# A fused attention, gated and slot-expert kernel: another load plan, other hand-over steps in the last pass, another order of the tail

## The chip, the cores and the metric

The kernel runs on one core of a Trainium2 chip as one launch. The metric is device time in microseconds (us) of an execution. Engines are named as in the profile: PE (matmul; PEld is its weight load), DVE (vector), ACT (scalar), POOL (GpSimd) and SP, which here only issues DMAs.

## What is computed

Three layers in a chain, all in fp32, cut from the reference (4 sequences of 448 rows, 12 heads of 64, so 1792 tokens of width 768):

```python
# 1 talking-heads attention: heads are mixed before and after the softmax
scores = scale * q @ k.T                       # (4, 12, 448, 448)
scores = einsum('bhij,hg->bgij', scores, w_pre)
attn = softmax(scores)                         # max subtracted, EPS in the sum
attn = einsum('bhij,hg->bgij', attn, w_post)
x = (attn @ v)                                 # -> (1792, 768)
# 2 gated layer; its weights come as 64-bit floats
h = x @ w_in                                   # (1792, 2048)
x = (h - tanh(h)) @ w_out
# 3 soft mixture: 8 experts of 4 slots each
logits = x @ phi                               # (1792, 32)
slot_in = softmax(logits, axis=0).T @ x        # (32, 768)
for e in range(8):
    h = relu(slot_in[e] @ w1[e])               # w1[e]: 768 x 1024
    slot_out[e] = h @ w2[e]                    # w2[e]: 1024 x 768
out = softmax(logits, axis=1) @ slot_out       # (1792, 768)
```

## The kernel before, in words

**Attention (talking_heads, to about 450 us).** The rows of scores are cut into 16 chunks (120, 120, 120 and 88 rows a sequence) and those into 184 steps of up to ten rows. Scores of a chunk go to a tile S; SP then fetches the rows of one step over all heads into a tile D (L312, 210 KB), four steps ahead of its use, into six buffers. Every second step PE mixes two D by w_pre (pm, L321), ACT makes the exponentials, and PE mixes and transposes them back (tm, L364). SP's other DMAs are written into a plan, at steps of their own: loads of k, q and v (load_k, load_q, load_v) and the conversion of w_in and w_out from 64-bit floats to fp32 in 56 pieces (load of 384 KB, arithmetic on ACT, DVE and POOL, store of 192 KB). The plan keeps a tally of work per step: `fetch` gives a load a span of steps and a cost, and the load goes to the step with the least tally of "dma" around it; `due` spreads the conversion pieces. SP issues in the order of the steps, all on one queue.

**Gated layer (moe_and_slots, to about 790 us).** Four passes over the tokens (512, 512, 512 and 256), each with 16 steps (NF), one per 128 columns of h. A step is 18 matmuls hp (L831) in six groups (c = 0 to 5); other work hangs on these groups as hooks, `on(c, ...)`, where KD = 6 means behind the last. A step's h goes through ACT and DVE (gate_act, gate_first, gate_last; result g), and turn_g transposes the g of two steps before (PE gt, ACT copy) into a quad buffer; the quads of a pass are summed over the tokens by the slot weights es (slot_sum, PE sp) in the pass that follows. logits, mix_t, slot_exp and slot_turn make es. LAST is the first step of the last pass.

**Buffers for expert weights.** Each of 32 loads of 1536 KB needs a home; `give` adds one to the list and `load_expert` fills it, in the order of `queue`. In the last pass homes come free as tiles of the gated layer are done with: two at its start, three at step 5 (two ring buffers of the weights and three quads, released together), one at step 14; loads there are cut into pieces (load_piece), one or two a step. After the pass every home comes from a load that PE has used up.

**Tail.** Behind the last pass stand the last gates, slot sum, the slot inputs (si), their transposes (sip, from every sixth column) and the experts: hidden(e) makes h, finish(e) copies h (ACT), transposes it (tz, from every eighth column) and takes the maximum with 0; slot_out(e, part) adds to so in two banks, one per half of the output columns. Five experts load w2 in two parts by rows, three (by_column) by halves of the columns, these last of all. slot_mix makes S4 of a half, output(hf) multiplies 14 tiles of 128 tokens and stores them in groups of four, four, four and two (768, 768, 768 and 384 KB).

## Time and profile before

| | us |
|---|---|
| median of three runs | 896.32 (896.07 to 898.48) |
| profiled execution, its own time | 903.9 |
| span of the profiled execution, first to last instruction | 902.1 |
| PE busy in the span | 828.4 |
| DVE, ACT, POOL busy | 554.9, 572.7, 249.0 |

The profile is one execution with the hardware profiler on, so its time is compared with its own parts, and the runs' median with other runs. A wait is the idle time of an engine just before an instruction, put down to what ended it. The clock is the share of full speed that TensorE was granted, the DMA share the mean busy share of 16 DMA engines.

### The profile page before, as it was taken

The numbers are of one execution on the slowest core, as the hardware profiler recorded it, in microseconds if no ns is written. First come the engines' busy times: TensorE is split into PE (matmuls) and PEld (weight loads), VectorE is DVE, ScalarE is ACT, GpSimd is POOL, SyncE is SP. The second block draws the span as 40 slices with busy tenths as digits, with TensorE's granted clock in tenths as the row PEclk, the third lists the DMA queues.
The fourth block names the chain that finished last, engine by engine and source line by source line (L and its number), as shares of the span: only waits on it lengthen the run. The fifth ranks groups of instructions, "written<-read, shape, count | busy, mean of one in ns | idle before, by whom it ended". The sixth has DMA issues, their size and how long they took to land.

```text
span 902.1 us, 28586 instructions
## 1 busy us (share of the span) xinstructions
PE 828.4 (92%) x11760; PEld 586.2 (65%) x11760; DVE 554.9 (62%) x1177; ACT 572.7 (63%) x1347; POOL 249.0 (28%) x430
## 2 busy tenths in 40 slices
PE   8878988989988898989999999999999999999995
PEld 6556665656655666766776767767776777964543
DVE  4456766658667576858467886566766776820104
ACT  4757877768877688878666775546664666820013
POOL 6244334424433344434303453000000003700000
PEclk9979999989999999999999999999999999997997
DMA  6889888886898877875669976588755456999997
GB/s 137 225 210 234 229 214 222 224 222 205 217 213 226 225 215 205 246 211 180 203 217 362 379 270 211 199 312 325 300 210 175 161 183 225 319 382 419 416 371 255
DMA packets 145590, 224.53 MB, mean 249 GB/s; under 512 B 60916, under 2 KB 126516, under 8 KB 142132
## 3 DMA queue, kind: packets, MB, share of 16 engines
q1 hardware_dynamic: 142112, 209.83, 74.6%
q10 hardware_dynamic: 3348, 12.87, 3.7%
q8 instruction: 93, 1.52, 0.7%
q14 instruction: 37, 0.30, 0.1%
HBM read 147.96 MB, written 36.18 MB: 204 GB/s over the span
## 4 chain that ended last, share of the span: by engine, by line
PE 61%; DMA 13%; ACT 10%; DVE 8%; issue 6%; SPq 1%; POOL 1%; ACTq 0%; POOLq 0%; DVEq 0%
PE hp L831 21%; DMA D<-S 9%; PE pm L321 6%; PE tm L364 5%; PE sc L287 5%; PE vx L403 4%; ACT e L333 4%; PE h L1320 3%; DVE mx L325 3%; PE gt L902 2%; PE so L1361 2%; PE tz L1340 2%; PE lgp L986 2%; ACT S L295 2%; PE sp L1068 1%
## 5 line engine op out<-in xcount | busy, mean ns | idle before, releaser
L333 ACT ACTIVATE e<-pm,mx 128x448 f32<-128x448 f32 x184 | 115.2, 631 | 89.1 <-DVE mx L325 85.7
L325 DVE TENSOR_REDUCE mx<-pm 128x1 f32<-128x448 f32 x184 | 106.1, 618 | 83.1 <-PE pm L321 83.0
L831 PE MATMUL hp<-xa,rg 128*128 128x512 f32 x576 | 153.0, 405 | 0.6 <-ACT xa L814 0.4
L364 PEld LDWEIGHTS tm<-wk,e 64*56 64x56 f32 x5888 | 111.8, 132 | 59.4 <-issue 37.0
L321 PE MATMUL pm<-D,wpre 64*64 64x448 f32 (+2 forms) x736 | 117.0, 573 | 20.6 <-DMA D<-S 18.1
L364 PE MATMUL tm<-wk,e 64*56 64x60 f32 x5888 | 121.1, 220 | 12.9 <-issue 11.1
L831 PEld LDWEIGHTS hp<-xa,rg 128*128 128x128 f32 x576 | 102.3, 188 | 29.9 <-issue 10.5
L295 ACT ACTIVATE S<-sc 120x448 f32<-120x448 f32 (+1 forms) x186 | 91.4, 551 | 14.2 <-DMA D<-S 5.3
L287 PE MATMUL sc<-khi,qT 64*120 64x448 f32 (+1 forms) x384 | 84.1, 399 | 8.8 <-DVE xs L413 5.5
L339 POOL TENSOR_SCALAR rv<-ss 128x2 f32<-128x2 f32 x92 | 24.5, 266 | 238.1 <-ACT e L333 207.9
L350 POOL TENSOR_SCALAR wk<-wpost,rv 128x60 f32<-128x60 f32 x184 | 85.3, 494 | 16.2 <-DVE rv L343 14.8
L403 PE MATMUL vx<-aT,vn 128*64 128x120 f32 (+1 forms) x1536 | 86.1, 265 | 1.9 <-issue 1.4
L788 POOL TENSOR_TENSOR rg<-rg 128x384 fp32r<-128x384 f32 x24 | 24.0, 1013 | 209.4 <-DVE rg L785 200.4
L403 PEld LDWEIGHTS vx<-aT,vn 128*64 128x64 f32 x1536 | 75.6, 139 | 8.8 <-issue 4.0
L378 ACT ACTIVATE aT<-tm 128x480 f32<-128x480 f32 x144 | 75.9, 592 | 2.2 <-PE tm L364 2.2
L851 ACT ACTIVATE sq<-hp 128x512 f32<-128x512 f32 (+1 forms) x62 | 32.8, 529 | 68.8 <-PE hp L831 68.7
L862 DVE SCALAR_TENSOR_TENSOR qd<-qd,sq 128x512 f32<-128x512 f32 (+1 forms) x61 | 37.6, 616 | 61.7 <-ACT mk L858 53.8
L831 PE MATMUL hp<-xb,rg 128*128 128x512 f32 x288 | 74.8, 405 | 0.0
L321 PEld LDWEIGHTS pm<-D,wpre 64*64 64x64 f32 (+2 forms) x736 | 25.8, 133 | 59.7 <-DMA D<-S 23.2
L287 PEld LDWEIGHTS sc<-khi,qT 64*120 64x120 f32 (+1 forms) x384 | 46.6, 177 | 25.5 <-PE tm L364 8.0
L831 PEld LDWEIGHTS hp<-xb,rg 128*128 128x128 f32 x288 | 52.0, 188 | 16.6 <-issue 6.3
L71 POOL TENSOR_TENSOR fa<-fa,f 128x384 f32<-128x384 f32 x56 | 57.4, 1025 | 7.2 <-DVE rv L343 3.4
(198 smaller groups left out, 1403.6 us busy)
## 6 DMA issues: line engine op xcount, KB each, us to landing
ex<-in_moe_w_dram SPq DMA_DIRECT2D x24, 1536.0 KB
D<-S SPq DMA_DIRECT2D x144, 210.0 KB
rg<-wis SPq DMA_DIRECT2D x36, 768.0 KB
f<-in_moe_w_in_dram SPq DMA_DIRECT2D x32, 384.0 KB
wis<-rg ACTq DMA_DIRECT2D x16, 768.0 KB
f<-in_moe_w_out_dram SPq DMA_DIRECT2D x24, 384.0 KB
rg<-wi SPq DMA_DIRECT2D x19, 384.0 KB
wi<-fa SPq DMA_DIRECT2D x32, 192.0 KB
```

Of the source, the lines that this page charges most:

```text
L71: eng.tensor_tensor(out=out, in0=bits(a), in1=bits(p), op=ALU.add)
L287: nc.tensor.matmul(xs[e][0][:ni], lhsT=qT[n][s, l, p, :ni], rhs=kt[s], start=(i == 0), stop=(i == 2))
L295: nc.scalar.activation(out=dst, in_=xs[e][0][:ni], func=ACTF.Copy)
L321: nc.tensor.matmul(xs[x][64 * i:64 * i + 64], lhsT=wpre[k0:k1], rhs=d[i][k0:k1], start=True, stop=True)
L325: nc.vector.tensor_reduce(out=mx[:, x:x + 1], in_=xs[x], op=ALU.max, axis=AX.X, negate=True)
L333: nc.scalar.activation(out=es[x], in_=xs[x], func=ACTF.Exp, bias=mx[:, x:x + 1], accum_out=ss[:, x:x + 1])
L350: nc.gpsimd.tensor_scalar(out=wk, in0=wpost, scalar1=rv[:, x:x + 1], scalar2=None, op0=ALU.mult)
L364: nc.tensor.matmul(xs[i][64 * z:64 * z + JH, x, c], lhsT=es[x][h, j:j + JH], rhs=wks[x][h], start=True, stop=True)
L378: nc.scalar.activation(out=out[:, :, c0:c0 + m].rearrange("p a (x i) -> p a x i", x=2), in_=x, func=ACTF.Copy)
L403: nc.tensor.matmul(x[64 * e:64 * e + 64, i, :ni], lhsT=nat_v[b, h // NP][:, h % NP, c, :], rhs=a[:, c, h, :ni], start=(c == 0), stop=(c == ...
L831: nc.tensor.matmul(hp, lhsT=r32(w[:, m, hl, cs]), rhs=r32(x_of(b, c, l)), start=(c == 0 and i == 0), stop=(c == KD - 1 and i == 2))
L862: nc.vector.scalar_tensor_tensor(out=qd, in0=qd, scalar=TG_E, in1=sq, op0=ALU.add, op1=ALU.mult)
```

## The change

Four things. The plan of attention's loads is made anew: all fetches are placed first and with larger costs, and the conversion pieces get due steps from the rest. In the last pass the ring buffers (one tile now) come free at step 3 and the quads at step 4, with slot sums, logits and one turn_g moved among the hooks; six experts load w2 by rows and two by columns. The transposes tz and sip read contiguous columns, since ACT and DVE write their sources in the other order (w2's rows are counted to suit). And the tail's order is new: slot_mix and output are generators that are taken forward in parts.

The diff, cut to its core:

```diff
-                fetch(max(t - 30, 3), t - 6, 0.45, load_k, chunks[m + 1][0], p)
+                fetch(max(t - 30, 3), t - 6, 1.3, load_k, chunks[m + 1][0], p)
-            fetch(max(2, t0 - 12), t0 - 8 if t0 > 12 else max(2, t0 - 7), 0.7, load_q, m)
+            fetch(max(2, t0 - 12), t0 - 8 if t0 > 12 else max(2, t0 - 7), 2.0, load_q, m)
+    for b in range(NB):
+        s0 = start[b * NC // NB]
+        fetch(s0 - 12 if b else 4, s0 + 8 if b else 13, 2.7, load_v, b, 0)
+        fetch(s0 + (T_LAG + 10 if b else 8), s0 + 15, 2.7, load_v, b, 1)
...
     pieces = box["early"]
+    first, last = 2, NS - D_AHEAD - 17
+    taken = [sum(load["dma"][:s + 1]) for s in range(NS)]
+    rate = (taken[last] + 2.1 * len(pieces)) / (last - first)
+    dues = []
+    for i in range(len(pieces)):
+        s = next(s for s in range(first, NS) if s >= last or taken[s] + 2.1 * (i + 1) <= rate * (s - first + 1))
+        dues.append((s + first + i * (last - first) // len(pieces)) // 2 + 6)
...
-        due = 6 + i * (NS - D_AHEAD - 17) // len(pieces)
+        due = dues[i]
...
-    rgs = [xep.tile([128, RU], FP32, tag=f"rg{i}", name="rg") for i in range(2)]
+    rgs = rgp.tile([128, 2 * RU], FP32, tag="rgs", name="rg")
...
+    def by_column(e):
+        return e >= NE - 2
...
-    def by_column(e):
-        return e >= NE - 3
...
-                src = w2[e].rearrange("(p a) f -> p a f", p=128)
+                src = w2[e].rearrange("(h p a) f -> p h a f", h=2, p=128)
...
+        elif kind == "e" and part > 1 and by_column(e):
+            for h in range(2):
+                nc.sync.dma_start(out=dst[:, h * (n // 2):(h + 1) * (n // 2)], in_=src[:, h])
...
-        on(4 if t > LAST + 2 else 2, turn_g, u)
+        on(5 if t == LAST + 1 else 4 if t > LAST + 2 else 2, turn_g, u)
...
-            on(3, logits, b - 1, NQ - 1)
-            on(4, logits_out, b - 1)
+            on(3 if b < NPASS - 1 else 5, logits, b - 1, NQ - 1)
+            on(4 if b < NPASS - 1 else 5, logits_out, b - 1)
...
-        if b and f in (4, 5):
+        if b == NPASS - 1 and f in (3, 4):
+            on(KD, slot_sum, b - 1, 2 * f - 6, 2 * f - 4)
+        elif 0 < b < NPASS - 1 and f in (4, 5):
             on(3, slot_sum, b - 1, 2 * f - 8, 2 * f - 6)
...
-            if f == 5:
+            if f == 3:
+                give(rgp.tile([128, EXB], FP32, tag="rgs", name="ex"))
+            if f == 4:
                 firsts.close()
                 zp = whole.enter_context(tc.tile_pool(name="m_z", bufs=1, reuse_waits="tile"))
-                for i in range(3):
+                for i in range(2):
                     give(zp.tile([128, EXB], FP32, tag=f"z{i}", name="ex"))
...
-            load_piece(2 if f < 5 or f > NF - 3 else 1)
+            load_piece(2 if f < 4 or f > NF - 3 else 1)
...
-    nc.vector.tensor_copy(out=siS[:, :HALF], in_=si[0])
-    nc.scalar.activation(out=siS[:, HALF:], in_=si[1], func=ACTF.Copy)
+    siS = siS.rearrange("p (c m) -> p c m", c=KD)
+    nc.vector.tensor_copy(out=siS[:, :, :64], in_=si[0].rearrange("p (m c) -> p c m", c=KD))
+    nc.scalar.activation(out=siS[:, :, 64:], in_=si[1].rearrange("p (m c) -> p c m", c=KD), func=ACTF.Copy)
...
-        nc.tensor.matmul(sp[:, c, :], lhsT=siS[:, c::KD], rhs=seld, start=True, stop=True)
+        nc.tensor.matmul(sp[:, c, :], lhsT=siS[:, c], rhs=seld, start=True, stop=True)
...
-        nc.scalar.activation(out=hs, in_=hp, func=ACTF.Copy)
+        nc.scalar.activation(
+            out=hs.rearrange("p (a m) -> p a m", m=128), in_=hp.rearrange("p (m a) -> p a m", m=128), func=ACTF.Copy)
...
-        for fc in range(KF1):
-            for hf in range(2):
-                nc.tensor.matmul(
-                    tz[64 * hf:64 * hf + 64, fc, :], lhsT=hs[:, fc::KF1], rhs=sela[:, e, hf, :],
-                    start=True, stop=True)
+        for a in range(n):
+            nc.tensor.matmul(
+                tz[:, a].rearrange("p h s -> p (h s)"), lhsT=hs[:, a * 128:(a + 1) * 128],
+                rhs=sela[:, e].rearrange("p h s -> p (h s)"), start=True, stop=True)
...
-        nc.scalar.activation(out=s4[0:64], in_=x[0:64], func=ACTF.Copy)
+        nc.vector.tensor_copy(out=s4[0:64], in_=x[0:64])
...
-    slot_mix(0)
-    slot_out(NE - 3, 1)
-    output(0)
+    mix = slot_mix(0)
+    next(mix)
+    idle = p1.tile([128, 128], FP32, tag="h1", name="warm")
+    for _ in range(3):
+        nc.tensor.matmul(idle, lhsT=ident, rhs=ident, start=True, stop=True)
+    next(mix)
     slot_out(NE - 2, 1)
+    part = output(0, (OG, OG, OG, 2))
+    for _ in range(2 * OG):
+        next(part)
     slot_out(NE - 1, 1)
-    slot_mix(1)
-    output(1)
+    mix = slot_mix(1)
+    next(mix)
+    for _ in range(OG):
+        next(part)
+    next(mix)
+    for part in (part, output(1, (2, OG, OG, OG))):
+        for _ in part:
+            pass
```

**The order on SP, at the start of attention.** D<-S rows are the fetches for the steps, kn, qn and vn loads of k, q and v, and f loads of conversion pieces. Before:

```order
L312 DMA D<-S 120x1x448 x7
L94 DMA f_436<-in_moe_w_in_dram 128x3x256
L312 DMA D<-S 120x1x448
L88 DMA f_461<-in_moe_w_out_dram 128x768
L164 DMA kn<-in_k_dram 112x8x64
L312 DMA D<-S 120x1x448 x2
L94 DMA f_519<-in_moe_w_in_dram 128x3x256
L180 DMA qn<-in_q_dram 88x12x64
L312 DMA D<-S 120x1x448 x2
L174 DMA vn<-in_v_dram 56x6x256 x2
L312 DMA D<-S 120x1x448 x2
```

And of the change, for the same fetches:

```order
L312 DMA D<-S 120x1x448 x7
L180 DMA qn<-in_q_dram 88x12x64
L312 DMA D<-S 120x1x448 x2
L174 DMA vn<-in_v_dram 56x6x256 x2
L312 DMA D<-S 120x1x448 x2
L164 DMA kn<-in_k_dram 112x8x64
L312 DMA D<-S 120x1x448 x2
```

Ahead of the 13th fetch stood three conversion loads, one k, one q and a pair of v; of these the conversion loads now come later. Farther on, the pair of v that stood behind the 97th fetch stands behind the 87th.

**The order on PE, in the first steps of the last pass.** hp<-xc are its products, gt the transposes of turn_g, lgp the logits, lT mix_t. Before:

```order
L831 MATMUL hp<-xc,rg 128x256 x6
L902 MATMUL gt<-ident,g 128x128 x4
L831 MATMUL hp<-xc,rg 128x256 x18
L902 MATMUL gt<-ident,g 128x128 x4
L831 MATMUL hp<-xc,rg 128x256 x3
L986 MATMUL lgp<-g,wphi 32x512 x4
L831 MATMUL hp<-xc,rg 128x256 x12
L997 MATMUL lT<-lp,sel 128x512
```

And of the change:

```order
L841 MATMUL hp<-xc,rg 128x256 x6
L912 MATMUL gt<-ident,g 128x128 x4
L841 MATMUL hp<-xc,rg 128x256 x27
L912 MATMUL gt<-ident,g 128x128 x4
L996 MATMUL lgp<-g,wphi 32x512 x4
L841 MATMUL hp<-xc,rg 128x256 x6
L1007 MATMUL lT<-lp,sel 128x512
```

Nine products stand ahead of the second gt that stood behind it, and the logits follow it at once.

**The order on PE, from expert 6's turns to the end.** tz are the turns, so the slot outputs, s the slot mix, op the output tiles. Before:

```order
L1340 MATMUL tz<-sela,tq 64x4 x16
L1320 MATMUL h_11942<-ex,siT 32x512 x12
L1340 MATMUL tz<-sela,tq 64x4 x16
L1361 MATMUL so<-ex,tq 32x384 x8
L1361 MATMUL so<-tq 32x384 x8
L1400 MATMUL s_11992<-ex,sel 128x384
L1361 MATMUL so<-ex,siT 32x384 x8
L1417 MATMUL op<-C4T 128x384 x14
L1361 MATMUL so<-ex,tq 32x384 x16
L1400 MATMUL s_12068<-ex,sel 128x384
L1417 MATMUL op<-C4T 128x384 x14
```

And of the change:

```order
L1356 MATMUL tz<-sela,tq 128x8 x4
L1335 MATMUL h_11869<-ex,siT 32x512 x12
L1356 MATMUL tz<-sela,tq 128x8 x4
L1378 MATMUL so<-tq 32x384 x8
L1378 MATMUL so<-ex,tq 32x384 x8
L1458 MATMUL warm<-ident 128x128 x3
L1419 MATMUL s_11911<-ex,sel 128x384
L1378 MATMUL so<-ex,tq 32x384 x8
L1434 MATMUL op<-C4T 128x384 x8
L1378 MATMUL so<-ex,tq 32x384 x8
L1434 MATMUL op<-C4T 128x384 x4
L1419 MATMUL s_11972<-ex,sel 128x384
```

The turns fall from 16 matmuls to four, one part of so stands behind the first mix where expert 5's second half stood, and the last part of so stands between output tiles; behind the last row 16 tiles follow in one row.

## Rows read from the trace of the kernel before

**Rows 1.** The page's chain that ended last: shares by engine, then by line.

```profile
PE 61%; DMA 13%; ACT 10%; DVE 8%; issue 6%; SPq 1%; POOL 1%; ACTq 0%; POOLq 0%; DVEq 0%
PE hp L831 21%; DMA D<-S 9%; PE pm L321 6%; PE tm L364 5%; PE sc L287 5%; PE vx L403 4%; ACT e L333 4%; PE h L1320 3%; DVE mx L325 3%; PE gt L902 2%; PE so L1361 2%; PE tz L1340 2%; PE lgp L986 2%; ACT S L295 2%; PE sp L1068 1%
```

**Rows 2.** PE's waits, 20 to 66 us: total us, times, longest.

```profile
PE pm L321 <- DMA D<-S: 7.0, 7, 2.9
```

**Rows 3.** PE's waits, 115 to 195 us.

```profile
PE pm L321 <- DMA D<-S: 6.3, 4, 2.2
```

**Rows 4.** PE's waits, 250 to 300 us.

```profile
PE pm L321 <- DMA D<-S: 4.9, 8, 0.9
```

**Rows 5.** Windows in attention: length, busy us (instructions) by engine, clock, DMA share, GB/s.

```profile
20.00:66.00 46.00, 37.40 (x619) 22.88 (x623) 20.93 (x48) 31.32 (x80) 18.12 (x43) 0.89 0.86 219
...
250.00:300.00 50.00, 41.59 (x925) 28.64 (x925) 30.43 (x72) 33.63 (x87) 18.77 (x36) 0.99 0.89 221
```

**Rows 6.** PE in order of time, 738 to 748: start, us, instructions, idle before.

```profile
739.67 2.38 PE L831 MATMUL hp<-xc,rg 128*128 128x256 f32 x18
743.62 0.66 PE L902 MATMUL gt<-ident,g 128*128 128x128 f32 x4 [1.57 <-DVE g L876]
```

**Rows 7.** Windows of the last pass and of the expert weights.

```profile
754.00:764.00 10.00, 9.68 (x81) 5.79 (x81) 6.97 (x21) 5.94 (x17) 4.88 (x6) 1.00 0.32 101
...
804.00:854.00 50.00, 49.22 (x506) 25.50 (x500) 4.75 (x16) 4.07 (x8) 1.75 (x6) 0.90 1.01 417
854.00:879.50 25.50, 23.78 (x260) 12.23 (x252) 1.13 (x4) 4.72 (x9) 0.56 (x2) 0.93 1.05 370
```

**Rows 8.** PE in order of time, 812 to 840: the experts.

```profile
812.27 5.35 PE L1320 MATMUL h<-ex,siT 128*32 128x512 f32 x24
...
832.03 2.76 PE L1361 MATMUL so<-ex,tq 128*32 128x384 f32 x32
...
836.74 2.78 PE L1320 MATMUL h<-ex,siT 128*32 128x512 f32 x24
839.34 1.47 PE L1361 MATMUL so<-tq 128*32 128x384 f32 x16
```

**Rows 9.** Windows behind the last weights.

```profile
879.50:882.00 2.50, 2.15 (x16) 1.24 (x8) 1.86 (x4) 0.97 (x3) 0.00 (x0) 1.00 0.32 110
882.00:884.00 2.00, 1.97 (x12) 0.93 (x12) 1.86 (x5) 1.81 (x4) 0.00 (x0) 1.00 0.68 248
...
890.00:894.00 4.00, 3.98 (x12) 3.29 (x12) 2.79 (x5) 2.22 (x5) 0.00 (x0) 0.50 0.26 98
```

**Rows 10.** All engines in order of time, 753 to 755: PE's products and es.

```profile
753.00 2.05 PE L831 MATMUL hp<-xc,rg 128*128 128x256 f32 x15
...
754.38 0.28 ACT L1058 ACTIVATE es<-etp 128x128 f32<-128x128 f32 x1
```

**Rows 11.** A window of 2 us at the last pass's end.

```profile
786.00:788.00 2.00, 2.00 (x19) 2.00 (x18) 1.40 (x4) 1.83 (x6) 1.28 (x2) 1.00 0.65 254
```

**Rows 12.** Instructions by line, 786 to 902: busy us, mean ns, idle before.

```profile
L1340 PE MATMUL tz<-sela,tq 128*64 128x4 f32 x256 | 16.7, 263 | 1.6 <-ACT tq L1328 1.6
...
L1328 ACT ACTIVATE tq<-h 128x512 f32<-128x512 f32 x8 | 4.8, 597 | 45.8 <-PE h L1320 45.8
...
L1297 PE MATMUL sip<-seld,tq 128*128 128x32 f32 x12 | 2.9, 392 | 0.0
...
L1387 PE MATMUL ctp<-ident,ex 128*128 128x128 f32 x14 | 2.0, 285 | 0.3 <-ACT C4T L1390 0.3
```

**Rows 13.** The page's groups by line: the strided copy out of PSUM.

```profile
L378 ACT ACTIVATE aT<-tm 128x480 f32<-128x480 f32 x144 | 75.9, 592 | 2.2 <-PE tm L364 2.2
```

**Rows 14.** PE in order of time, 872 to 880.

```profile
872.48 2.79 PE L1361 MATMUL so<-ex,tq 128*32 128x384 f32 x16
...
878.41 1.50 PE L1361 MATMUL so<-ex,siT 128*32 128x384 f32 x16
```

**Rows 15.** A window of 2 us in the first expert's h.

```profile
814.00:816.00 2.00, 2.00 (x16) 0.57 (x12) 0.07 (x1) 0.00 (x0) 0.00 (x0) 0.50 0.96 375
```

More of the change, by code (lines that the diff above doesn't have):

```diff
@@ L482, in talking_heads, with crowd @@
             job(calm("pe", lo, lo + step - 1) if m + 2 < NC else lo, values, m, g, dve=0.41, pe=2.0)
-    pieces = box["early"]
+    for b in range(NB):
+        s0 = start[b * NC // NB]
+        fetch(s0 - 12 if b else 4, s0 + 8 if b else 13, 2.7, load_v, b, 0)
+        fetch(s0 + (T_LAG + 10 if b else 8), s0 + 15, 2.7, load_v, b, 1)
+    def crowd(s):
+        return sum(load["dma"][max(s - 1, 0):s + 2]), s
+    for hi, lo, cost, f, a in sorted(wanted, key=lambda z: (z[0] - z[1], z[0])):
+        s = min(range(lo, hi + 1), key=crowd)
+        load["dma"][s] += cost
+        plan("load", s, f, *a)
+    pieces = box["early"]
+    first, last = 2, NS - D_AHEAD - 17
[5 more added lines that the diff above has]
+        dues.append((s + first + i * (last - first) // len(pieces)) // 2 + 6)
     done = [0] * cv.bufs
@@ L500, in talking_heads @@
         plan("load", at_load, cv.load, j)
-        load["dma"][at_load] += 0.4
+        load["dma"][at_load] += 1.5
         plan("act", a, cv.absolute, j)
@@ L506, in talking_heads @@
         plan("load", e + 4, cv.store, j)
-        load["dma"][e + 4] += 0.2
-    for b in range(NB):
-        s0 = start[b * NC // NB]
-        fetch(s0 - 12 if b else 4, s0 + 8, 0.8, load_v, b, 0)
-        fetch(s0 + (T_LAG + 10 if b else 8), s0 + 15 if b else 13, 0.8, load_v, b, 1)
-    def crowd(s):
-        return sum(load["dma"][max(s - 1, 0):s + 2]), s
-    for hi, lo, cost, f, a in sorted(wanted, key=lambda z: (z[0] - z[1], z[0])):
-        s = min(range(lo, hi + 1), key=crowd)
-        load["dma"][s] += cost
-        plan("load", s, f, *a)
+        load["dma"][e + 4] += 0.6
     pre_rows = rows_of("wpre", w_pre, ((4, 2 * IH),))
@@ L704, in moe_and_slots @@
         queue += [("e", 4 * e + 4), ("e", 4 * e + 5)]
-        if e < NE - 3:
+        if not by_column(e):
             queue += [("e", 4 * e + 2), ("e", 4 * e + 3)]
-    queue += [("e", 4 * e + i) for i in (2, 3) for e in range(NE - 3, NE)]
+    queue += [("e", 4 * e + i) for i in (2, 3) for e in range(NE) if by_column(e)]
     def give(x, last=False):
@@ L1336, in finish @@
                 slot_out(beside, 1)
-        tz = p1.tile([128, KF1, SPE], FP32, tag="ht", name="tz")
-        for fc in range(KF1):
-            for hf in range(2):
-                nc.tensor.matmul(
-                    tz[64 * hf:64 * hf + 64, fc, :], lhsT=hs[:, fc::KF1], rhs=sela[:, e, hf, :],
-                    start=True, stop=True)
+        n = KF1 // 2
+        tz = p1.tile([128, n, 2, SPE], FP32, tag="ht", name="tz")
+        for a in range(n):
+            nc.tensor.matmul(
+                tz[:, a].rearrange("p h s -> p (h s)"), lhsT=hs[:, a * 128:(a + 1) * 128],
+                rhs=sela[:, e].rearrange("p h s -> p (h s)"), start=True, stop=True)
         nc.vector.tensor_scalar(
-            out=hts[e][:, :, e * SPE:(e + 1) * SPE], in0=tz, scalar1=0.0, scalar2=None, op0=ALU.max)
+            out=hts[e].rearrange("p (h a) s -> p a h s", h=2)[:, :, :, e * SPE:(e + 1) * SPE], in0=tz, scalar1=0.0,
+            scalar2=None, op0=ALU.max)
         if e == NE - 1:
@@ L1396, in slot_mix @@
         n = NT + hf * HALF
-        s4, s4h = mem["ct"][:, n:n + HALF], mem["ct"][:, EXB - HALF:]
+        s4 = mem["ct"][:, n:n + HALF]
+        s4h = r32(tt[:, hf * HALF:(hf + 1) * HALF])
         nc.vector.tensor_copy(out=ss, in_=so[hf])
+        yield
         x = p1.tile([128, HALF], FP32, tag="h1", name="s4")
@@ L1401, in slot_mix, with output @@
         nc.scalar.activation(out=s4h[64:128], in_=x[64:128], func=ACTF.Copy)
-        nc.scalar.activation(out=s4[0:64], in_=x[0:64], func=ACTF.Copy)
+        nc.vector.tensor_copy(out=s4[0:64], in_=x[0:64])
         nc.vector.tensor_tensor(out=s4[64:128], in0=x[64:128], in1=bits(s4h[64:128]), op=ALU.subtract)
         S4[hf] = s4
-    def output(hf):
+        yield
+    def output(hf, groups):
         hs = slice(hf * HALF, (hf + 1) * HALF)
-        t1 = 0
-        while t1 < NT // 128:
-            t0 = t1
-            n = min(NT // 128 - t0, OG)
-            t1 = t0 + n
+        t = 0
+        for n in groups:
             o = spare().rearrange("p (t d) -> p t d", d=HALF)
+            t0 = t
             for i in range(n):
-                t = t0 + i
                 x = p1.tile([128, HALF], FP32, tag="s" if t % 2 else "ht", name="op")
@@ L1421, in output @@
                     nc.vector.tensor_copy(out=o[:, i, :], in_=x)
-            nc.sync.dma_start(
-                out=out[t0 * 128:(t0 + n) * 128, hs].rearrange("(t p) d -> p t d", p=128), in_=o[:, :n, :])
+                t += 1
+                if i == n - 1:
+                    nc.sync.dma_start(
+                        out=out[t0 * 128:t * 128, hs].rearrange("(t p) d -> p t d", p=128), in_=o[:, :n, :])
+                yield
     finish(0, hidden(0))
```

6 lines of the change are left out of this document (3 added, 3 removed).

## The prediction

> **What bounds the kernel now.** I read the page's chain first: PE carries 61% of it, DMA 13%, and most of DMA's part is D<-S [rows 1]. So I looked for the places where PE stands, and then for those where PE works but something else sets the end.
>
> The attention stage (0 to 450 us) is PE's, with waits for D, the regrouped scores that SP fetches four steps ahead. They come in three crowds: 7.0 us in 20 to 66, 6.3 us in 115 to 195, 4.9 us in 250 to 300 [rows 2 to 4]. The DMA share there is 0.86 and 0.89 at some 220 GB/s [rows 5]: D stands in the queue behind loads. After 340 no wait for D is listed.
>
> The last pass (738 to 790) is PE's too; its one stall of size is 1.57 us at the transposes gt, which wait for g from DVE [rows 6]. The DMA engines are almost empty there for 10 us, share 0.32 in 754 to 764 [rows 7].
>
> After 790 comes the stream of expert weights, and the DMA engines are full until 879.5: share 1.01, then 1.05 [rows 7]. PE is busy as well (49.2 of 50 us in 804 to 854), so the chain names PE. But PE works through a stock of buffers that DMA fills at half PE's pace: an expert takes PE 7.31 us (so at 832.03, the next at 839.34 [rows 8]), and DMA four loads of 1536 KB, each 1.573 MB / 417 GB/s = 3.8 us, so 15 us. The stock falls until the last loads land at about 879.5. Behind that, in 22.6 us, the output goes out: 2 x (3 x 768 + 384) KB = 5.5 MB, 14.9 us at 370 GB/s. In three gaps the DMA engines are idle instead: 2.5 x 0.68 + 2.0 x 0.32 + 4.0 x 0.74 = 5.3 us [rows 9]. The other 2.4 us are the end behind the last packets and slower stretches; I keep them.
>
> **The change, part by part.**
>
> *Load plan.* On SP three conversion loads (384 KB each) that stood ahead of the 13th D now come later, 1152 KB or 1.18 MB. At 219 GB/s [rows 5] that is 5.4 us less queue ahead of one of the Ds for which PE waits in the first crowd. Bounds there: nothing, and all of the 7.0 us. What PE no longer waits is also time in which the queue no longer drains, so I take 4.0 us.
> What leaves the first crowd must be carried later, since pieces and sizes are the same. In the second crowd the order shows me no shift worth a number. In the third a pair of v loads (2 x 336 KB, 0.69 MB, 3.1 us at 221 GB/s) goes ten steps forward, from the 97th D to the 87th, in among the next batch's loads of k. D's slack shrinks there first, but by the crowd's end as much has been carried as before. Bounds: a gain of the whole 4.9 us, and a loss of 5 (that pair and one conversion load, 1.8 us, both late); I take a loss of 2.0. Loads that fall behind 340 have cover, as PE waits for no D there. Net: -2.0 us, between -11.9 and +5.
>
> *Last pass.* turn_g of the step LAST+1 moves behind three more groups of products: nine matmuls, at 2.38 us / 18 = 0.13 each [rows 6], put 1.2 us of PE work into the 1.57 us stall. The slot sums move half a step forward, to the ends of steps 3 and 4. They need es, which ACT finishes at 754.66. Of the 15 products from 753.00 on only six now stand ahead of the sums, so PE is there at 753.8 [rows 10] and waits up to 0.9 us: ACT's queue holds the gate's instructions ahead of es. Behind the sums stand only the next products, late by as much. Sum: -0.4 us (bounds -1.6 and +0.9).
>
> *Buffers handed over at steps 3 and 4.* This sounds like the cure for the empty 10 us, and I cost it at almost nothing. The homes are as many as before (one and two, where three came at step 5), pieces go out one a step, and in 786 to 788 the DMA share is 0.65 before too [rows 11]: whatever had a home was nearly loaded when the next home came. At most one piece of 384 KB more is ahead, 0.9 us; I take 0.3.
>
> *Turns from contiguous rows.* tz falls from 16 matmuls to 4 an expert, in PE's rows (two a matmul) from 32 to 8. The 32 take 16.7 / 8 = 2.1 us. The nearest row for 128 contiguous columns is ctp, 14 in 2.0 us, 0.14 each [rows 12]; eight are 1.1. So 8 x 1.0 = 8.0 us less for PE. sip's twelve take 2.9 us; at ctp's pace 1.7, so 1.2 us less. A loss on PE has no reason, as no more columns are read than before. Together 9.2 us, **but beside a full DMA stream**: they are worth only what lets PE be there when the last weights land.
> What was strided on PE is now strided in ACT's read of PSUM. L1328 takes 0.60 us for 512 contiguous columns [rows 12], and L378 reads 480 in another order in 0.59 [rows 13], so I take no loss. The Trainium skill (SBUF — State Buffer, "Door 1: The DMA port swizzle") says that PSUM has lines of 8 bytes and that a pattern with gaps is slow there; by that the copy might double. Six of the eight copies lie beside so (2.6 us), so the rule would cost 0.6 to 1.2 us and the row costs nothing; no trace yet shows a read of every fourth column.
>
> *Two experts by column, not three.* Halves of columns are loaded at 370 GB/s, whole rows at 417 [rows 7]. Two loads change: 2 x (4.25 - 3.77) = 1.0 us. Last landing: 879.5 - 1.0 - 0.3 = 878.2.
>
> *Order of the tail.* Counted back in steps of 4.25 us, the last four loads land at about 865.5, 869.7, 874.0 and 878.2. PE, 9.2 us ahead of its 872.5 [rows 14], is there before each from the second on: DMA is the new bound, and any more speed on PE is lost. Two groups of output now stand ahead of the last part of so, so 1.6 MB are queued when the weights end, and a third is made ahead of the second mix. That covers the gaps of 879.5 to 884, and the third gap shrinks as one of the mix's two ACT copies moves to DVE beside the other. I leave 1.0 of the 5.3 us idle. The last group is larger (768 KB, 2.2 us) but issued at about 890, before the queue is empty. End: 878.2 + 22.6 - 4.3 = 896.5, **-5.6** on 902.1 (bounds -7.5, no idle at all and a whole piece ahead, and -2).
>
> Sum: -2.0 - 0.4 - 5.6 = -8.0 us, a span of 894.1. The profiled execution took 903.9 us with a span of 902.1, and the median of the runs is 896.32; I carry the difference over: 896.3 - 8.0 = **888.3 us**.
>
> **The rivals.**
>
> *The plan moves its crowd.* For it: the DMA share is high in the crowds [rows 5], so little can be smoothed, and slack used early is missing later. Against: no D waits behind 340. With +3 in place of -2 the end is 893.3.
>
> *The tail stays short of DMA.* PE now stands between landings, and its clock may fall: 16 matmuls of so took 2.79 us at 872.48 and 1.50 at 878.41 [rows 14]. Then 3.5 us of idle DMA stay: 890.8.
>
> *More than I grant.* The first and third crowds go (-9 for -2), or the hand-over does fill the empty 10 us (6.8 us of DMA): 881 to 882. Against the second stands the count of homes.
>
> *Slower: the clock of the expert stage.* h took 5.35 us at 812.27, where 0.50 was granted (1.2 GHz), and 2.78 at 836.74 [rows 8, 15], so a whole expert (h and so) at the lower level costs PE some 5.2 us more. PE has 9 us in hand against DMA; from the second such expert on it sets the end again, and five of them would give 888.3 + 26 - 9 = 905. For it: the clock did fall there, behind the small matmuls of sip. Against: in 829 to 842 each h, so and tz kept its pace, with more small ones. The Trainium skill (TensorE: Matmul & The Clock Gate, "HAM oscillation — how this bites in real kernels") describes kernels that fall to the slow level at each wait for DMA; here that could strike only where PE waits, behind 865.
>
> **How the numbers follow.** My forecast with its own range, 885 to 891.5, has 0.56. One of the two losses (891.5 to 893.6) has 0.18, more than I grant 0.13, both losses together (895.8, no change that can be measured) 0.08, slower 0.05. What a measurement can tell from no change is 0.3%, 2.7 us, so faster means below 893.6: 0.87, 0.08 and 0.05. The range of 881.5 to 894 leaves out a part of the first and most of the last two.
>
> **What would show it.** D waits of about 3 us in 20 to 66 and 5 to 8 us in 240 to 300. No wait of gt for DVE in the second step of the last pass, but one of sp for es. DMA share near 1 from 790 to the end but for some 1 us; waits of so for its weights in the last three parts; tz at about 1 us. I am wrong if the third crowd passes 10 us, if the weights' end moves by much more or less than the earlier stages and 1.3 us, or if h takes over 4 us behind the second expert.

## The result and the profile after

The changed kernel took 888.52 us (median of four runs, 886.33 to 889.92) where the kernel before took 897.4 on the same chip: ratio 0.9895, 95% interval 0.9857 to 0.9933. The forecast was 888.3. On another chip, twelve runs gave 892.51 against 897.02: 0.9935, 0.9899 to 0.9970. A run more than 1.5% above the fastest of its kernel counts as slow and is left out of the ratio, though not of the median. So the gain is 8.9 and 4.5 us by medians, 9.4 and 5.8 by ratios, and the forecast of 8.0 lies between; but one kernel's runs spread over 13 us there (882.67 to 896.12), and so the stages are compared in several executions below.

The profiled execution took 886.33 us (span 884.6), the fastest of its four; the one before ([rows 1 to 15]) was slower than all its runs. Their difference, 17.5 us, is not the gain.

The page's part on the chain, of the changed kernel:

```profile
## 4 chain that ended last, share of the span: by engine, by line
PE 51%; DMA 20%; ACT 12%; DVE 9%; issue 5%; SPq 1%; POOL 1%; ACTq 0%; POOLq 0%; DVEq 0%
PE hp L841 21%; DMA D<-S 9%; DMA ex<-in_moe_w_dram 6%; PE pm L321 5%; PE sc L287 5%; ACT e L333 4%; PE tm L364 4%; PE vx L403 4%; DVE mx L325 3%; ACT S L295 2%; PE gt L912 2%; ACT aT L378 2%; DMA rg<-wi 2%; PE sp L1078 1%; PE lgp L996 1%
```

PE has given ten points to others ([rows 1]); new is DMA of expert weights with 6%: PE now waits for them. The waits of PE, by stretch: 20 to 66 and 235 to 295 us (they answer to [rows 2, 4]).

```profile
PE pm L321 <- DMA D<-S: 8.2, 5, 3.8
...
PE pm L321 <- DMA D<-S: 1.5, 1, 1.5
```

In this execution the first crowd didn't shrink (7.0 before) and the third did. One execution can't carry that: the changed kernel's second profile (after_again, below) has in 20 to 66 us

```profile
PE pm L321 <- DMA D<-S: 2.1, 2, 1.8
```

Over the ten executions of the table below, the waits of pm for D in the first three stretches of attention sum to 6.4, 4.9 and 3.4 us on average with the old plan (three executions) and to 6.3, 5.1 and 3.8 with the new one (seven). No crowd shrank by the plan. Now the stretches of attention, cut at the first pm of steps 0, 24, 84 and 132, and at the last pm; first the kernel before, then the changed one (columns: length, busy time and count of PE, PEld, DVE, ACT and POOL, granted clock, DMA share, GB/s):

```profile
21.70:80.30 58.60, 48.78 (x896) 31.49 (x896) 31.52 (x73) 41.79 (x107) 22.60 (x52) 0.91 0.90 220
80.30:228.00 147.70, 131.97 (x2940) 93.90 (x2938) 101.24 (x233) 113.33 (x296) 57.67 (x112) 0.97 0.82 221
228.00:346.80 118.80, 103.24 (x2321) 73.47 (x2319) 79.70 (x184) 89.04 (x234) 45.82 (x89) 0.99 0.84 216
346.80:448.60 101.80, 94.72 (x2381) 68.77 (x2381) 69.11 (x161) 81.36 (x222) 41.36 (x88) 0.98 0.70 207
```

```profile
21.50:77.50 56.00, 45.07 (x895) 29.78 (x895) 24.89 (x58) 40.07 (x104) 18.70 (x49) 0.94 0.88 208
77.50:218.20 140.70, 126.64 (x2938) 90.33 (x2934) 100.11 (x233) 113.12 (x296) 58.18 (x112) 1.00 0.84 227
218.20:332.50 114.30, 103.87 (x2320) 73.84 (x2316) 78.17 (x185) 88.71 (x235) 45.73 (x87) 0.96 0.85 227
332.50:435.60 103.10, 93.13 (x2377) 67.58 (x2380) 75.73 (x176) 82.77 (x225) 47.84 (x93) 0.98 0.74 220
```

Length times rate is what was carried: 12.9 MB in the first stretch before and 11.7 after (the 1.18 MB of the prediction), 21.1 and 22.7 in the last. The plan has moved data to the end, and there the stretch is longer. The arithmetic of the conversion moved along: in the last stretch DVE is busy for 75.7 us where it was 69.1, and POOL for 47.8 where it was 41.4.

In the last pass and the expert stage of the changed kernel (PE's rows, in order of time; the number in brackets is the wait ahead, and for what):

```profile
730.78 0.66 PE L912 MATMUL gt<-ident,g 128*128 128x128 f32 x4 [0.51 <-DVE g L886]
...
740.78 0.62 PE L1078 MATMUL sp<-tq,es 128*32 128x512 f32 x1 [0.71 <-ACT es L1068]
...
795.52 1.53 PE L1312 MATMUL sip<-seld,tq 128*128 128x32 f32 x12
...
797.52 2.78 PE L1335 MATMUL h<-ex,siT 128*32 128x512 f32 x24
...
844.58 2.66 PE L1378 MATMUL so<-ex,siT 128*32 128x384 f32 x16 [2.10 <-DMA ex<-in_moe_w_dram]
847.17 1.88 PE L1356 MATMUL tz<-sela,tq 128*128 128x8 f32 x8
848.98 5.00 PE L1335 MATMUL h<-ex,siT 128*32 128x512 f32 x24
854.74 1.06 PE L1356 MATMUL tz<-sela,tq 128*128 128x8 f32 x8 [0.76 <-ACT tq L1343]
```

And one row of PE's weight loads (PEld), inside the h of 848.98:

```profile
852.07 0.16 PEld L1335 LDWEIGHTS h<-ex,siT 128*32 128x32 f32 x8 [1.20 <-DMA ex<-in_moe_w_dram]
```

The stall of gt fell from 1.57 to 0.51 and sp got one of 0.71: minus 1.06 plus 0.71. tz takes 1.06, sip 1.53 (2.88 before), and the h that took 5.35 ([rows 8]) takes 2.78. PE waits for weights six times from 840 on, and behind such a wait one h (848.98) took 5.00 us: its first half ran at a granted clock of 0.50 (1.2 GHz; the row of 846 to 850 below), and in its middle its weight loads waited 1.20 us for DMA. The DMA share stayed at 1 beside it. The windows of that stretch:

```profile
777.00:791.00 14.00, 12.89 (x108) 9.01 (x111) 4.93 (x16) 3.68 (x12) 0.00 (x0) 1.00 1.01 400
791.00:841.00 50.00, 47.09 (x462) 21.98 (x455) 5.02 (x17) 7.21 (x14) 2.32 (x8) 1.00 1.00 410
841.00:856.00 15.00, 12.14 (x76) 4.90 (x80) 0.28 (x2) 0.60 (x1) 0.00 (x0) 0.77 1.02 397
846.00:850.00 4.00, 4.00 (x24) 2.15 (x18) 0.19 (x1) 0.00 (x0) 0.00 (x0) 0.50 0.98 400
856.00:866.50 10.50, 7.07 (x60) 2.61 (x52) 2.37 (x6) 0.91 (x3) 0.00 (x0) 1.00 1.00 352
866.50:870.00 3.50, 3.12 (x23) 1.38 (x24) 1.77 (x4) 1.39 (x4) 0.00 (x0) 1.00 0.67 239
870.00:876.00 6.00, 4.60 (x19) 2.62 (x17) 5.28 (x11) 4.03 (x9) 0.00 (x0) 1.00 1.02 362
```

DMA is full up to 866.5, and one gap of 1.2 us (3.5 x 0.33) is left of three ([rows 9]). From 866.5 to the end at 884.6 it is 18.1 us, where it was 22.6. From the first si on, the stage took 95.5 us (99.9 before).

### The profile page after: what moved, and what is told of

Same layout as the page of the kernel before. It is cut to its first block, busy times and chain, and to the rows that moved or that the text cites. A ratio compares the mean times of both kernels' runs of the same rounds, so it can differ in the third digit from the quotient of the medians.

```text
span 884.6 us, 28215 instructions
## 1 busy us (share of the span) xinstructions
PE 807.4 (91%) x11574; PEld 568.8 (64%) x11574; DVE 553.0 (63%) x1179; ACT 570.6 (65%) x1345; POOL 252.2 (29%) x430
## 4 chain that ended last, share of the span: by engine, by line
PE 51%; DMA 20%; ACT 12%; DVE 9%; issue 5%; SPq 1%; POOL 1%; ACTq 0%; POOLq 0%; DVEq 0%
PE hp L841 21%; DMA D<-S 9%; DMA ex<-in_moe_w_dram 6%; PE pm L321 5%; PE sc L287 5%; ACT e L333 4%; PE tm L364 4%; PE vx L403 4%; DVE mx L325 3%; ACT S L295 2%; PE gt L912 2%; ACT aT L378 2%; DMA rg<-wi 2%; PE sp L1078 1%; PE lgp L996 1%
## 5 line engine op out<-in xcount | busy, mean ns | idle before, releaser
L364 PEld LDWEIGHTS tm<-wk,e 64*56 64x56 f32 x5888 | 108.4, 130 | 61.3 <-issue 33.3
L364 PE MATMUL tm<-wk,e 64*56 64x60 f32 x5888 | 116.0, 218 | 12.9 <-issue 8.6
L321 PE MATMUL pm<-D,wpre 64*64 64x448 f32 (+2 forms) x736 | 111.0, 574 | 18.2 <-DMA D<-S 11.9
L841 PEld LDWEIGHTS hp<-xa,rg 128*128 128x128 f32 x576 | 102.2, 188 | 30.1 <-issue 10.5
L350 POOL TENSOR_SCALAR wk<-wpost,rv 128x60 f32<-128x60 f32 x184 | 87.9, 506 | 15.9 <-DVE rv L343 12.6
L403 PE MATMUL vx<-aT,vn 128*64 128x120 f32 (+1 forms) x1536 | 84.3, 262 | 3.7 <-issue 3.3
L841 PEld LDWEIGHTS hp<-xb,rg 128*128 128x128 f32 x288 | 52.0, 188 | 16.6 <-issue 6.3
```

Source lines behind the costliest of these rows:

```text
L321: nc.tensor.matmul(xs[x][64 * i:64 * i + 64], lhsT=wpre[k0:k1], rhs=d[i][k0:k1], start=True, stop=True)
L350: nc.gpsimd.tensor_scalar(out=wk, in0=wpost, scalar1=rv[:, x:x + 1], scalar2=None, op0=ALU.mult)
L364: nc.tensor.matmul(xs[i][64 * z:64 * z + JH, x, c], lhsT=es[x][h, j:j + JH], rhs=wks[x][h], start=True, stop=True)
L403: nc.tensor.matmul(x[64 * e:64 * e + 64, i, :ni], lhsT=nat_v[b, h // NP][:, h % NP, c, :], rhs=a[:, c, h, :ni], start=(c == 0), stop=(c == ...
L841: nc.tensor.matmul(hp, lhsT=r32(w[:, m, hl, cs]), rhs=r32(x_of(b, c, l)), start=(c == 0 and i == 0), stop=(c == KD - 1 and i == 2))
```

## The experiments

Twelve runs. Each stage below is read from the profile of its run: attention from first to last pm, its four stretches cut as above; from the last pass's first hp to the first si; from that si to the last packet of weights; behind that packet, and how much of it DMA was idle; from si to the end. (That last packet lies 1.5 to 2 us behind the end of the full share, which the prediction took as landing.) All in us; the ratio to the kernel before, over the same chip's runs, stands at the right.

| run | attention | its four stretches | pass to si | si to last weights | behind them (idle) | si to end | ratio, 95% interval |
|---|---|---|---|---|---|---|---|
| before | 426.9 | 58.6, 147.7, 118.8, 101.8 | 63.6 | 79.2 | 20.7 (5.2) | 99.9 | |
| before_again | 419.4 | 58.5, 147.8, 116.5, 96.6 | 63.5 | 79.2 | 18.8 (3.3) | 97.9 | |
| plan_only | 417.4 | 55.6, 143.3, 115.7, 102.7 | 64.2 | 79.7 | 19.6 (4.1) | 99.4 | 0.9975, 0.9947 to 1.0003 |
| old_plan | 415.3 | 58.4, 143.9, 113.3, 99.7 | 63.4 | 79.4 | 16.6 (1.2) | 96.0 | 0.9986, 0.9952 to 1.0020 |
| changed | 414.2 | 56.1, 140.7, 114.3, 103.1 | 63.4 | 78.9 | 16.6 (1.2) | 95.5 | 0.9895, 0.9857 to 0.9933 |
| after_again | 419.9 | 57.5, 143.3, 113.8, 105.3 | 64.0 | 77.9 | 16.6 (1.3) | 94.6 | 0.9935, 0.9899 to 0.9970 |
| old_tail | 418.3 | 56.4, 144.5, 114.0, 103.4 | 63.9 | 78.6 | 19.8 (4.4) | 98.4 | 0.9975, 0.9949 to 1.0002 |
| old_turns | 415.7 | 56.1, 141.3, 115.4, 102.9 | 64.3 | 78.2 | 17.4 (2.0) | 95.7 | 0.9983, 0.9950 to 1.0016 |
| old_hand | 418.3 | 57.1, 140.8, 115.3, 105.1 | 63.7 | 79.4 | 16.8 (1.4) | 96.2 | 0.9945, 0.9921 to 0.9970 |
| three_col | 418.4 | 56.1, 142.8, 114.2, 105.3 | 62.4 | 79.5 | 16.7 (1.3) | 96.2 | 0.9935, 0.9905 to 0.9966 |

Four kernels more, on the first crowd, stand further down.

**The two kernels once more.**

> The changed kernel once more, on the same chip as the three that each undo one part of it: they are to be compared with this run. Expected 0.990 of before (-8.9 us, as measured), and in a second profiled execution the lengths of the stages behind attention as in the first: 50.5 us of last pass, 95.5 us from the first instruction of si to the end. The attention stage may differ by several us between two executions.

> The kernel before, once more, for a second profile: its first one was of an execution 6.5 us slower than its own median. If the stage behind si is long by the program, it is again some 99.9 us there, and the attention stage is 415 to 420 us, as in the changed kernel with the old plan (415.3 us from first to last pm). If the 13 us of attention were the plan's, it is again near 427 us.

Behind attention it is as expected, within 1 us (pass to si 64.0, stage 94.6); the gain isn't: 4.5 us by medians (ratio 0.9935) where 8.9 (0.990) was expected. The kernel before took 419.4 us of attention this time, and 97.9 behind si: the first profile of it was long in both. So the 13 us of attention between the first two profiles can't be put down to the plan (two executions of the kernel before alone differ by 7.5, two of the changed one by 5.7), and 2 of the 4.4 us behind si were not the change's.

**The plan.** plan_only is the kernel before with the new plan, old_plan the changed kernel with the old one:

```diff
-                fetch(max(t - 30, 3), t - 6, 1.3, load_k, chunks[m + 1][0], p)
+                fetch(max(t - 30, 3), t - 6, 0.45, load_k, chunks[m + 1][0], p)
...
-        due = dues[i]
+        due = 6 + i * (NS - D_AHEAD - 17) // len(pieces)
```

> The kernel before with the new load plan alone. By the prediction's term: 2.0 us faster than before. By the difference between the changed kernel and the changed kernel with the old plan (892.51 against 895.78 us): 3.3 us faster. Rival, the plan does nothing and executions of attention merely differ: 0.

> The changed kernel with the old plan of attention's loads, all else as changed. By the prediction's sum the plan is worth 2.0 us, so this one is 2.0 us slower than the changed kernel and 6.7 us faster than before. By the trace of the changed kernel (attention 13 us shorter in an execution that was among the fastest, against one that was among the slowest) it is worth more: 4 to 5 us, so 4 to 5 us faster than before. By the rival in which the plan only moves its crowd it is as fast as the changed kernel or up to 3 us faster.

plan_only: 895.27 against 897.39, 2.1 us. old_plan: 895.78, 3.3 us more than the changed kernel on its chip. The first interval still takes in no change, and those of old_plan and the changed kernel overlap. The stretches tell more. Means of the three executions with the old plan (before, before_again, old_plan) and of the seven with the new one: 58.5 and 56.4, 146.5 and 142.4, 116.2 and 114.7, 99.4 and 104.0. In the first and the last, every execution of one plan lies on the same side of every one of the other. The plan gains 7.7 us up to step 132 and gives 4.6 back behind it: 3.1 net. But this net rests on the first profile of the kernel before: without it the same sums are 5.7 gained and 5.8 given back, and nothing is left. That time was moved is shown; that some is saved rests on the two differences of medians.

**The tail's order.** old_tail puts it back, and with it the mix's copies on ACT and the old groups of output tiles:

```diff
-    part = output(0, (OG, OG, OG, 2))
-    for _ in range(2 * OG):
-        next(part)
+    output(0)
+    slot_out(NE - 2, 1)
     slot_out(NE - 1, 1)
-    mix = slot_mix(1)
...
+    slot_mix(1)
+    output(1)
```

> The changed kernel with the old order behind the last weights: second halves of so, mix and output one after the other, both copies of the mix on ACT, groups of 4, 4, 4 and 2 tiles in both halves. By the prediction's term (the idle time of the DMA engines behind the last landing, 5.3 us down to 1.0) it is 4.3 us slower than the changed kernel, and the gaps of DMA come back: three of 2 to 4 us behind the last weights. Rival: the gaps went because PE is earlier there by its faster turns, not by the order; then it is less than 1 us slower.

Idle DMA behind the weights is back at 4.4 us and the stage at 98.4, 3.0 above the mean of the three with the new order and all else that bears on it (changed, after_again, old_plan: 95.4); its median is 2.5 us above the changed kernel's on the same chip, with intervals that overlap. So the new tail carries it, not PE's speed; which of its parts does was not tried. In windows behind the last weights, before, before_again, old_tail, then the changed kernel:

```profile
881.40:902.10 20.70, 11.27 (x58) 6.39 (x58) 7.87 (x15) 7.08 (x15) 0.00 (x0) 0.69 0.75 266
```

```profile
874.30:893.00 18.70, 8.67 (x54) 3.96 (x52) 6.33 (x12) 5.80 (x13) 0.00 (x0) 0.86 0.82 293
```

```profile
874.20:894.00 19.80, 9.93 (x54) 5.71 (x53) 6.81 (x13) 6.21 (x13) 0.00 (x0) 0.76 0.78 278
```

```profile
868.00:884.60 16.60, 7.07 (x38) 3.56 (x30) 6.85 (x14) 5.40 (x12) 0.00 (x0) 0.83 0.93 330
```

DMA's share is 0.75, 0.82 and 0.78 with the old order and 0.93 with the new one. The first row is the one that the prediction knew: its clock was 0.69 there, 0.86 in the second execution of the same kernel, whose gaps are 1.9 us shorter. Whether the clock made them shorter isn't shown: plan_only at 0.86 has 4.1 us idle, and old_plan, with the new order, 1.2 at a clock of 0.71.

**The turns.** old_turns has tz in sixteen matmuls of every eighth column and sip of every sixth:

```diff
-        for a in range(n):
-            nc.tensor.matmul(
-                tz[:, a].rearrange("p h s -> p (h s)"), lhsT=hs[:, a * 128:(a + 1) * 128],
...
+        for fc in range(KF1):
+            for hf in range(2):
+                nc.tensor.matmul(
+                    tz[64 * hf:64 * hf + 64, fc, :], lhsT=hs[:, fc::KF1], rhs=sela[:, e, hf, :],
```

> The changed kernel with the old transposes: tz in sixteen matmuls of every eighth column, sip of every sixth column, w2 counted in the old way. PE has some 9 us more to do between si and the last weights. By the prediction this lies beside a full DMA stream: 0 to 1.5 us slower than the changed kernel, the last weights land within 1 us of the same distance from the start of si, and the waits of PE for weights are shorter by about as much as PE does more. Rival, PE carries the stage: 5 to 9 us slower, and the last weights land later by that.

Rows of lines from si to the end, old_turns first, then the changed kernel:

```profile
L1351 PE MATMUL tz<-sela,tq 128*64 128x4 f32 x256 | 16.7, 262 | 1.6 <-ACT tq L1339 1.6
...
L1308 PE MATMUL sip<-seld,tq 128*128 128x32 f32 x12 | 2.9, 388 | 0.0
```

```profile
L1356 PE MATMUL tz<-sela,tq 128*128 128x8 f32 x64 | 9.3, 272 | 1.5 <-ACT tq L1343 1.5
...
L1343 ACT ACTIVATE tq<-h 128x512 f32<-128x512 f32 x8 | 4.8, 597 | 46.0 <-PE h L1335 46.0
...
L1312 PE MATMUL sip<-seld,tq 128*128 128x32 f32 x12 | 1.5, 278 | 0.0
```

PE does 8.8 us more in old_turns, waits 0.3 us for weights in place of 7.7 ([rows 12] have the same times as its rows), and the stage takes 95.7 us in place of 95.5 and 94.6. The median is 1.7 us above the changed kernel's, with intervals that overlap widely. PE's gain there was swallowed whole, as forecast.

**The hand-over and the columns.**

```diff
-            if f == 3:
-                give(rgp.tile([128, EXB], FP32, tag="rgs", name="ex"))
-            if f == 4:
+            if f == 5:
...
-                for i in range(2):
+                for i in range(3):
```

> The changed kernel with the old hand-over: ring buffers and quads given to the experts together at step 5 of the last pass, slot sums, logits and turn_g on their old hooks. By the prediction's terms (0.4 for the pass, 0.3 for the landing) 0.7 us slower than the changed kernel: gt waits 1.6 us for g again, sp no longer waits for es, and the last weights land within 1 us of the same distance from the start of si. Rival, earlier homes fill the empty time of DMA in the last pass: the last weights land 3 us or more later, behind the same start of si.

```diff
-        return e >= NE - 2
+        return e >= NE - 3
...
+    slot_out(NE - 3, 1)
     slot_out(NE - 2, 1)
```

> The changed kernel with three experts by column, as before, all else as changed. By the prediction's term (two loads of 4.25 us in place of 3.77) the last weights land 1.0 us later behind the start of si: 79.2 to 79.5 us in place of 77.9 to 78.9, and the stage from si to the end is some 96.0 us in place of 94.6 to 95.5. Rival: rows or columns make no difference to a full stream; then both stay.

old_hand: the median is that of after_again to the digit (892.51). gt waits 1.57 us again and sp no more. The last weights come at 79.4, later than in the changed kernel by 0.5 and 1.5; but old_plan, with the new hand-over, has 79.4 too. So no 3 us, and whether 0.3 or 1 stays open. three_col: 79.5 and 96.2, 1.1 us above the means of changed and after_again, as expected, though old_plan (79.4) shows that one execution can't hold such a difference. Its ratio (0.9935) is that of after_again.

**What stands in the first crowd.** The plan took conversion loads out of it, and its waits stayed. act_conv has the conversion loads on ACT's queue; v_early has the first batch's v loads ahead of the first step:

```diff
-            self.nc.sync.dma_start(
+            self.nc.scalar.dma_start(
```

> The changed kernel with the 56 conversion loads of attention (384 KB each) issued by ACT, on its own queue, at the same places of the plan; everything else as changed. Theory: D is late because it stands in SP's queue behind loads, and the clock falls behind such waits. Then PE's waits for D in attention fall from 12 to 13 us to under 4, fewer stretches there run at the lower clock, and the kernel is 6 to 15 us faster than the changed one. Rival: the 16 DMA engines are what is short in those stretches (share 0.83 to 0.9), whichever queue a load stands in; then the waits for D stay above 9 us and the time is that of the changed kernel within 2 us, or longer where ACT stands before a load whose buffer is not free.

```diff
         if p == 3:
             load_q(1)
+            load_v(0, 0)
+            load_v(0, 1)
...
+    for t in vns[:2]:
+        for z in range(2):
+            nc.gpsimd.memset(t[64 * z + 32:64 * z + 64], 0.0)
     wpre = kron("wpre", pre_rows, HD ** -0.5, True)
```

> The changed kernel with the four v loads of the first batch (4 x 336 KB, 1.38 MB) issued before the first step, behind the second q load, where the DMA engines stood almost idle (12 to 20 us), and the clearing of their tiles moved ahead on POOL; their places in the plan stay empty. Theory: the first crowd (8.2 us of waits for D in 20 to 66) did not shrink because v and k stand in it, not the conversion. Then its waits fall to 1 to 3 us, less of it runs at the lower clock, the first stretch is 6 to 11 us shorter, and the kernel is 5 to 10 us faster than the changed one (0.983 to 0.988 of before). Rival: conversion, k and q fill the place, the crowd moves on by some steps and the time is within 2 us of the changed kernel's. Second rival: wpre, now behind more work of POOL, or D, now behind v, delays the first pm by 1 us or more and that is lost.

> As v_early, and the 56 conversion loads on ACT's queue. If both queues' crowds are separate causes, it is 2 to 4 us faster than v_early alone (the conversion loads on ACT's queue gave 2.7 us by the medians of two calls, within their uncertainty); if the DMA engines are what is short, it is as fast as v_early within 1.5 us.

```diff
-    for t in vns[:2]:
-        for z in range(2):
-            nc.gpsimd.memset(t[64 * z + 32:64 * z + 64], 0.0)
     wpre = kron("wpre", pre_rows, HD ** -0.5, True)
+    for z in range(2):
+        nc.gpsimd.memset(vns[1][64 * z + 32:64 * z + 64], 0.0)
...
+    for z in range(2):
+        nc.vector.memset(vns[0][64 * z + 32:64 * z + 64], 0.0)
```

> As v_early_act, but the clearing of the first two v tiles no longer stands between the two instructions on POOL that make ident (there it delayed the first matmuls from 1.43 to 2.86 us, and the first pm from 21.5 to 23.4 us): one tile is cleared by DVE, one by POOL behind wpre. Theory: the late start was that order alone, so the first matmul is back at 1.4 us, the first pm at 21.5 to 22.5 us, waits for D in 15 to 66 stay under 3.5 us, and the kernel is 1 to 2 us faster than v_early_act, 0.981 to 0.984 of before. Rival: the start was late because v stands ahead of the first D in the queue; then the first pm stays at 23 us or later.

| run | first pm | first stretch | attention | si to end | median | ratio, 95% interval |
|---|---|---|---|---|---|---|
| act_conv | 21.6 | 55.6 | 417.9 | 94.8 | 889.78 | 0.9913, 0.9881 to 0.9944 |
| v_early | 24.1 | 51.8 | - | - | 890.06 | 0.9867, 0.9810 to 0.9923 |
| v_early_act | 23.4 | 52.7 | 414.4 | 95.7 | 884.96 | 0.9836, 0.9787 to 0.9886 |
| v_clear | 24.0 | 53.1 | 411.6 | 97.9 | 888.82 | 0.9880, 0.9826 to 0.9934 |

(v_early's profiled execution took 894.79 us, 4.7 over its median; only its first 80 us are used. Its ratio is that of four runs out of six.) Waits for D, act_conv in 20 to 66, then v_early, then v_clear, both in 15 to 66:

```profile
PE pm L321 <- DMA D<-S: 7.5, 5, 3.9
```

```profile
PE pm L323 <- DMA D<-S: 1.2, 2, 0.9
```

```profile
PE pm L323 <- DMA D<-S: 1.9, 3, 1.0
```

With the conversion on another queue the first crowd is as it was, and D waits in all of attention were 10.5 us, not under 4: that theory falls, at least for conversion loads. With v away the waits for D are 1.2, 3.2 (v_early_act) and 1.9 us, where nine of the ten executions in the first table have 5.5 to 8.4 in the first stretch (after_again alone has 2.1), and the stretch is shorter than in every one of them: v stood there (1.38 MB, 6.3 us at the 220 GB/s of [rows 5]). The place for it was free, as windows of 12 to 20 us show, the changed kernel, then v_early_act:

```profile
12.00:20.00 8.00, 7.16 (x67) 4.88 (x68) 5.54 (x11) 4.65 (x10) 7.73 (x10) 1.00 0.22 47
```

```profile
12.00:20.00 8.00, 7.31 (x71) 4.84 (x67) 5.60 (x10) 5.30 (x11) 5.16 (x8) 1.00 1.05 186
```

But the first pm starts 2 us later, and of some 4 us in the first stretch (6 to 11 were expected) about 2 are left. v_clear tells why: its first matmul is back at 1.42 us, and the first pm still at 24.0. Its first D is issued at 19.13 us, where it was 18.40 in the changed kernel, and pm waits for it 1.01 us (0.28 there); so 0.7 of the 2.6 us is the later issue, and for the rest the rival holds: the first D stands behind v. All three have ratios below the changed kernel's two, v_early_act the lowest, but their intervals overlap with each other and with that of 0.9895; v_clear was expected at 0.981 to 0.984 and has 0.9880. Which of them is best is open, and the stages explain some 2 us, not the 9 of v_early_act's ratio against 0.9935.

## Why the prediction was right, and where its steps were not

*Load plan, -2.0.* By the medians the term is about right, 2.1 and 3.3 us; by stretches it is 3.1 or nothing, with and without the first profile of the kernel before. Its working is not right. I took 4.0 off the first crowd because conversion loads left it; its waits stayed (6.4 us on average with the old plan, 6.3 with the new), as what filled it was v, though the stretch became 2.1 us shorter. I gave the second nothing and that stretch gained 4.1, and the third a loss of 2.0 where the stretch gained 1.5; their waits for D didn't fall either. So what the first three stretches gained isn't in the waits that I priced, and where it comes from was not separated: that the term came out near is luck. The step that failed outright is "Loads that fall behind 340 have cover": with the 1.6 MB more that are carried there, and the arithmetic that goes with them, that stretch took 4.6 us longer, and D has next to no part in it. In the changed kernel's waits from 332 to 436 us:

```profile
PE vx L403 <- issue: 3.3, 2, 2.4
PE tm L364 <- issue: 2.6, 1, 2.6
PE pm L321 <- ACT e L333: 1.5, 2, 0.8
PE tm L364 <- ACT aT L378: 1.1, 3, 0.5
```

"issue" over 0.1 us sums there to 4.0, 0.0 and 3.9 us with the old plan and to 3.2 to 5.8 with the new one, means 2.6 and 4.5; so it may be some 2 of the 4.6 us. The rest is spread over small waits and was not separated, nor was the part of the loads from that of the arithmetic. The rival "the plan moves its crowd" was half right, at another place.

*Last pass, -0.4.* gt's wait fell by 1.06 and sp's rose by 0.71, -0.35, as worked out. From the pass's start to si no difference shows above the spread (62.4 to 64.3): the four executions with the old hooks have 63.8 on average, the six with the new ones 63.6.

*Hand-over, 0.3, and columns, 1.0.* Over five executions with both changes (changed, after_again, old_plan, old_tail, old_turns) the last weights came 78.6 us behind si on average, over three without them 79.4: -0.8 for -1.3. The empty 10 us of the last pass were filled in part, but missing later: the windows have a share of 0.53 in 741 to 751 ([rows 7]: 0.32) and 0.48 in 772 to 776, and DMA was busy for some 40 us of the pass in the first two executions of either kernel. That fits the count of homes, which was worked out as the limit.

*Turns.* 8.8 us less PE for 9.2 forecast, worth nothing in the stage: old_turns. The copy that reads PSUM at every fourth column took 0.597 us where 0.60 was assumed. The Trainium skill (SBUF — State Buffer, "Door 1: The DMA port swizzle") says of PSUM that patterns with gaps slow down matmuls; that this copy might double was the prediction's estimate from it, and no such loss shows in this pattern.

*Order of the tail, -4.3.* Mechanism right, size off: idle DMA behind the weights fell from 5.2, 3.3 and 4.1 (three executions with the old order) to 1.2 and 1.3, so -3.0. I had costed it on one execution, the one with the longest gaps of the four with the old order (old_tail has 4.4). From si to the end the stage gained 3.7 (99.1, the mean of the same three, to 95.4), where the terms said 5.6. The rival in which 3.5 us of idle DMA stay didn't come.

*The slower rival,* the clock of the expert stage: the sign that I named for it, h over 4 us behind the second expert, came in the last expert of all six executions with the new turns (5.00 us at 848.98 in the changed kernel, 4.45 to 5.68 in the others). PE's first wait for weights came at 841, some 25 us ahead of their end (866.5), where I had named 13 (865 of 878). It didn't set the end: PE waited for weights around that h, in the changed kernel inside it too, and the stage is as long in old_turns (95.7), where every h behind the second took 2.78.

Worked anew: 2.1 to 3.3 for the plan by medians, 0.35, and 3.7 behind si (3.3 without the first profile of the kernel before) make 5.8 to 7.4 us, a ratio of 0.992 to 0.994 on 896.3, where 0.9895 and 0.9935 were measured. The runs of all parts but the plan, old_plan against before, give 1.2 us by medians and at most 4.3 by the interval, so the tail's 3.7 is at the edge of what they allow. On 896.3 the intervals of the two measurements are 883.5 to 890.3 and 887.3 to 893.6; the second holds the rivals' 890.8 and 893.3 as well as the forecast. That 888.3 came so near is in part luck: the tail was worth less than its 5.6, and the plan gave its share by another way than the one priced.

## What to carry to other kernels

Work that is moved out of one stage is not time gained until the stage that takes it is checked: here the last stretch of attention gave back most of what the first three gained. A crowd of waits in one profiled execution is not yet the kernel's: the changed kernel had 8.2 us in one and 2.1 in the next. Before a queue is smoothed, list what stands in it in the crowd by bytes: here it was v, and an idle stretch ahead of the loop had room for it, at the price of a later start. And price a gap from two profiled executions at least.
